# Narrower TensorE tiles, explicit PSUM banks, weights in long rows and a new written order in a retention-and-token-mixing kernel

## The chip, the cores and the metric

The kernel runs on one core of a Trainium2 chip. A core has a matrix engine (TensorE, PE in the profile, with its weight loads shown apart as PEld), a vector engine (DVE), a scalar engine (ACT), a general engine (GpSimd, POOL) and a sync engine (SP), which here only issues transfers. Sixteen DMA engines move data between HBM and SBUF. TensorE writes its results to PSUM, eight banks of 2 KB in each of 128 partitions, and DVE and ACT read them from there. Each engine works through its own queue in order, and waits for the others by semaphores. The metric is the device time of one launch in microseconds (us).

## The reference

The first half is a recurrent attention with decay (retention), for 4 batches, 8 heads, 768 steps and head width 64; the second half mixes tokens within a batch. Cut to what is computed:

```python
gamma = 1.0 - 2.0 ** (-5.0 - arange(H))
for t in range(S):
    state = gamma * state + outer(k[:, :, t], v[:, :, t])
    y[:, :, t] = (1/sqrt(D)) * q[:, :, t] @ state
x = y with heads side by side                    # [4, 768, 512]
wq = x @ w_q;  wk = x @ w_k                      # 512 -> 64 each
W_tok = (1/sqrt(64)) * wq @ wk.T                 # [768, 768] in each batch
out = relu(W_tok @ x) @ w_out                    # 512 -> 512
```

All inputs and the output are float32 in HBM: q, k and v of 6.29 MB each, 1.31 MB of weights, and 6.29 MB of output.

## The kernel before, in words

**Work units.** The 768 steps of a batch are cut into three pieces of 256 steps, called pairs (two chunks of 128), so there are twelve pairs, 0 to 11, three to a batch. Partition g of a tile holds two neighbouring steps, j = 0 and 1, and the eight heads are handled as two halves x = 0, 1 of four head pairs hp each. All matrix products take bfloat16 operands.

**Retention, for each pair p.** Transfers bring k, q and v in 512 KB pieces into staging tiles (`load`). `ck`, `cq` and `cv` turn them into bfloat16, the first two with the decay multiplied in (L253). `trk` and `trq` transpose k and q on TensorE, eight 128x128 transposes each, and `ekT`, `eqT` copy the result out of PSUM. `sc` makes the scores of half of the heads (16 matmuls on 64x64 tiles of the array, L316), and `eat` multiplies them by the causal mask on DVE (L329). `ia` applies the masked scores to v (L422). `st`, `X`, `Y` and `YS` add k times v into the state's PSUM bank and apply q to the state of the chunk before (L385), two streams of matmuls interleaved. `es` copies the state out. When the y of a pair is complete, `ex` copies it out of PSUM as x (L435).

**Token mixing.** W_tok is never formed: since W_tok @ x = wq @ (wk.T @ x), the kernel makes z = wk.T @ x once for each batch. `xt` and `exT` transpose x and copy it out. `wqk` makes wq (transposed, four matmuls of 256 columns, L460, with w_q in the stationary operand twice, so that the result stands on both halves of the partitions) and wk (eight matmuls of 64 columns, L470); `ew` copies both out. `zm` makes z from the three pairs of a batch (L492), so it can't run before the third pair's wk; `ez` copies it out. For each pair, `mx` multiplies z and wq (four matmuls of 256 columns, L514) into two banks, `r` applies the relu bank by bank (L529, L531), `pj` multiplies by w_out (four matmuls of 512 columns for each j, L538), and `eo` copies the result out for the store.

**Order.** The program's order is a written list of steps, ORDER (L17). A step's letter names its engine: A for ACT, V for DVE, P for POOL; steps without a letter are TensorE's. The list fixes the order within each engine's queue, and the framework adds the semaphores. `fill.n` puts n matmuls on zeros ahead of a step, whose result is overwritten; they keep TensorE busy. Loads and stores are both in SP's queue: the load of pair p+6 is issued when pair p's tile of the same name has been converted (`release`, L166), and the store of a pair where its second `eo` stands in the list. Both are in program order in that one queue. The three weight loads come after pair 2's loads (L159): w_q and w_k in 256-byte rows, w_out in rows of 2 KB.

**PSUM.** Of the eight banks, scores hold two, y two, the state one, and three rotate among all other results (L120 to L123).

Of the kernel before, what the change touches and what calls it, by code (L numbers as in the profile page):

```python
# [15 lines left out]

ORDER = """  # L17
fill.80 ck.0:V trk.0 cq.0:V ekT.0:A trq.0 cv.0:V fill.2 eqT.0:V
st.0 es.0.0:A sc.0.0 X.0 eat.0.0:V es.0.1:A sc.0.1 ck.1:P ia.0.0
eat.0.1:V cq.1:P Y.0 trk.1 fill.6 ekT.1:A ia.0.1 ex.0:V cv.1:P  # L20
trq.1 eqT.1:A xt.0 st.1 sc.1.0 exT.0:V ck.2:P es.1.0:A eat.1.0:V
X.1 es.1.1:A sc.1.1 cq.2:P trk.2 eat.1.1:V ia.1.0 ekT.2:V Y.1
ia.1.1 cv.2:A ex.1:V trq.2 st.2 fill.4 eqT.2:V xt.1 es.2.0:A
W:V sc.2.0 exT.1:A X.2 wqk.0 eat.2.0:V wqk.1 WO:A ew.0:V
sc.2.1 ew.1:V ia.2.0 eat.2.1:V ck.3:P Y.2 ia.2.1 ex.2:A cq.3:P
trk.3 xt.2 ekT.3:A fill.4 exT.2:V cv.3:A wqk.2 trq.3 ew.2:A
st.3 eqT.3:V zm.0 ck.4:P es.3.0:A ez.0:A X.3 sc.3.0 es.3.1:A
mx.0 eat.3.0:V r.0.1:A cq.4:P trk.4 r.0.0:A sc.3.1 ekT.4:A ia.3.0
eat.3.1:V mx.1 Y.3 r.1.0:A pj.0.0 cv.4:P r.1.1:A trq.4 fill.4
eo.0.0:A st.4 eqT.4:V ia.3.1 ck.5:P pj.0.1 ex.3:A es.4.0:V sc.4.0  # L30
eo.0.1:A X.4 eat.4.0:V xt.3 es.4.1:V cq.5:P trk.5 ekT.5:A exT.3:V
pj.1.0 sc.4.1 eo.1.0:A cv.5:P trq.5 eat.4.1:V ia.4.0 mx.2 eqT.5:A
YS.4 ia.4.1 es.5.0:A ck.6:P r.2.0:A ex.4:V wqk.3 trk.6 r.2.1:A
sc.5.0 pj.1.1 ew.3:A eat.5.0:V cq.6:P eo.1.1:A X.5 ekT.6:V ia.5.0
sc.5.1 cv.6:A xt.4 eat.5.1:V trq.6 pj.2.0 exT.4:A eqT.6:V ck.7:P
YS.5 eo.2.0:A sc.6.0 es.6.0:A ia.5.1 eat.6.0:V wqk.4 cq.7:P ex.5:A
pj.2.1 ew.4:A trk.7 eo.2.1:V xt.5 ekT.7:V sc.6.1 X.6 exT.5:V
cv.7:A eat.6.1:V trq.7 ia.6.0 eqT.7:A wqk.5 ck.8:P es.6.1:A sc.7.0
ew.5:V YS.6 eat.7.0:V es.7.0:A ia.6.1 zm.1 ex.6:A cq.8:P sc.7.1
ez.1:V X.7 eat.7.1:V trk.8 es.7.1:A xt.6 ekT.8:V cv.8:A ia.7.0  # L40
trq.8 exT.6:V Y.7 st.8 eqT.8:V mx.3 es.8.0:A ia.7.1 ck.9:P
r.3.1:A r.3.0:V sc.8.0 ex.7:V wqk.6 eat.8.0:V pj.3.0 ew.6:A cq.9:P
trk.9 eo.3.0:A pj.3.1 ekT.9:V X.8 eo.3.1:A cv.9:P mx.4 sc.8.1
r.4.0:A r.4.1:V trq.9 eat.8.1:V pj.4.0 eqT.9:A ck.10:P ia.8.0 eo.4.0:V
mx.5 YS.8 r.5.1:A r.5.0:V sc.9.0 ia.8.1 es.9.0:V pj.4.1 cq.10:P
ex.8:V trk.10 eo.4.1:A eat.9.0:V pj.5.0 ekT.10:A trq.10 cv.10:A eo.5.0:V
sc.9.1 X.9 eat.9.1:V ia.9.0 xt.8 ck.11:P xt.7 eqT.10:A exT.7:V
pj.5.1 exT.8:V wqk.7 es.9.1:V cq.11:P eo.5.1:A trk.11 ew.7:A wqk.8
YS.9 ew.8:V cv.11:P ekT.11:A sc.10.0 ia.9.1 es.10.0:A eat.10.0:V trq.11
ex.9:A zm.2 eqT.11:V X.10 ez.2:A sc.10.1 es.10.1:A ia.10.0 eat.10.1:V  # L50
mx.6 YS.10 r.6.0:A xt.9 es.11.0:A r.6.1:A sc.11.0 exT.9:V ia.10.1
mx.7 eat.11.0:V pj.6.0 r.7.0:A ex.10:V r.7.1:A wqk.9 eo.6.0:A pj.6.1
ew.9:A X.11 eo.6.1:A sc.11.1 ia.11.0 eat.11.1:V mx.8 pj.7.0 r.8.0:A
r.8.1:A Y.11 eo.7.0:V ia.11.1 pj.7.1 ex.11:A eo.7.1:A xt.10 xt.11
exT.10:V pj.8.0 exT.11:V wqk.10 eo.8.0:A wqk.11 ew.10:A pj.8.1 ew.11:A
zm.3 eo.8.1:A ez.3:A mx.9 r.9.0:A r.9.1:V mx.10 pj.9.0 r.10.1:A
r.10.0:V eo.9.0:V pj.9.1 mx.11 eo.9.1:A r.11.1:V r.11.0:A pj.10.0 eo.10.0:A
pj.10.1 eo.10.1:A pj.11.0 eo.11.0:A pj.11.1 eo.11.1:A
""".split()

STAGES = 6
# [3 lines left out]
def kernel(  # L65
# [10 lines left out]


# [10 lines left out]
    C = 128  # L88
# [15 lines left out]

# [3 lines left out]
    ost_pool = pool("ost", 7)  # L108
# [8 lines left out]
    moe_pool = pool("moe", 6)  # L117
    relu_pool = pool("relu", 2)
    PSUM = bass.MemoryType.PSUM
    at_psum = pool("at_psum", 1, space=PSUM)  # L120
    y_psum = pool("y_psum", 1, space=PSUM)
    s_psum = pool("s_psum", 1, space=PSUM)
    psum = pool("psum", 3, space=PSUM)  # L123

    pairs = [dict() for _ in range(NG)]
    state_ps = [None] * B
# [13 lines left out]
    def load(name, p):  # L140
        src = {"k": k, "q": q, "v": v}[name]
        b, cp = divmod(p, NP)
        t = stage_pool.tile([128, H, 2, D], FP32, name=name + "_st")
        eng = nc.scalar if (name, p) == ("k", 0) else nc.sync
        eng.dma_start(
            out=t.rearrange("g h j d -> g h (j d)"),
            in_=src[b, :, cp * 2 * C : (cp + 1) * 2 * C, :].rearrange(
                "h (g j) d -> g h (j d)", j=2
            ),
        )  # L150
        pairs[p][name + "_st"] = t

    wq_stage = wstage_pool.tile([128, NDM, DH], FP32, name="wq_stage")
    wk_stage = wstage_pool.tile([128, NDM, DH], FP32, name="wk_stage")
    wout_stage = wstage_pool.tile([128, NDM, DM], FP32, name="wout_stage")
    for p in range(STAGES):
        for name in "kqv":
            load(name, p)
        if p == 2:  # L159
            nc.sync.dma_start(out=wq_stage, in_=moe_w_q.rearrange("(a p) h -> p a h", p=128))  # L160
            nc.sync.dma_start(out=wk_stage, in_=moe_w_k.rearrange("(a p) h -> p a h", p=128))
            nc.sync.dma_start(
                out=wout_stage, in_=moe_w_out.rearrange("(a p) m -> p a m", p=128)
            )

    def release(name, p):  # L166

        if p + STAGES < NG:
            load(name, p + STAGES)
# [27 lines left out]

# [20 lines left out]
    wq_sb = const_pool.tile([128, NDM, 2, DH], BF16, name="wq_sb")  # L218
# [3 lines left out]
    def W(e):  # L222
        copy(
            e,
            wq_sb,
            wq_stage[:, :, None, :].to_broadcast([128, NDM, 2, DH]),
        )
        if e == "A":
            nc.scalar.mul(out=wk_sb, in_=wk_stage, mul=float(wk_scale))
        else:  # L230
            ENGINES[e].tensor_scalar_mul(out=wk_sb, in0=wk_stage, scalar1=float(wk_scale))
# [4 lines left out]


    fills = [0]

    def filled(dst):  # L240
        for i in range(fills[0]):
            if dst.dtype == BF16:
                nc.tensor.transpose(dst, warm, identity)  # L243
            else:
                nc.tensor.matmul(out=dst, lhsT=warm, rhs=warm, start=True, stop=True)
        fills[0] = 0
# [3 lines left out]
    def decay(e, p, name, table):  # L250
        st = pairs[p]
        st[name + "s"] = cast_pool.tile([128, HP, 2, 2, D], BF16, name=name + "s")
        ENGINES[e].tensor_tensor(  # L253
            out=st[name + "s"].rearrange("p hp j x d -> p x (hp j) d"),
            in0=st[name + "_st"].rearrange("p (x hp) j d -> p x (hp j) d", x=2),
            in1=table[:, p % NP]
            .rearrange("p (x hp) j -> p x (hp j)", x=2)
            .to_broadcast([128, 2, HP * 2, D]),
            op=ALU.mult,
        )  # L260
        release(name, p)

    def ck(e, p):
        decay(e, p, "k", fk)

    def cq(e, p):
        decay(e, p, "q", fq)
# [345 lines left out]
```

## Time and profile before

| | |
|---|---|
| median of 3 runs (lowest to highest) | 112.1 us (110.33 to 112.9) |
| profiled execution, its span | 109.7 us |
| what the span leaves to the median | 2.4 us |
| TensorE busy, weight loads busy | 93.8 us, 68.9 us |
| DVE, ACT, POOL busy | 64.9, 60.0, 49.4 us |
| moved by the DMA engines | 26.77 MB, mean 244 GB/s |
| first decay of pair 0's k starts | 6.46 us |
| decay of pair 3's k starts | 24.56 us |
| z of batch 0 ends on TensorE | 35.55 us |
| last matmul ends | 105.17 us |

The profile is of one execution, and its durations belong to the span of 109.7 us, from the first to the last instruction. The time of a run holds, beside the span, what lies around it: the median of the runs shown is 2.4 us above this span. In the profile, "L538" is a line of the kernel. A row of the groups gives the operation, the tile written and the tiles read, their sizes and how many; then busy time, the mean of one in ns, the engine's idle time just before them, and what ended that. The slices cut the span into 40 parts of 2.74 us; a digit is the busy share in tenths, for PEclk the granted TensorE clock. The chain is the work that ended last, followed back step by step. A row of the waits gives who waited, for what, the total in us, how often, and the longest.

The durations of the rows that are spoken of below, one instruction each: the decay of k or q 1.90 us on POOL and 1.22 on DVE; the mask multiply 1.22 (DVE); a copy of a whole transposed pair 1.02 (ACT) or 0.69 (DVE); `ex` 1.01 (ACT) or 1.22 (DVE), six on each; `es` 0.37 (ACT) or 0.41 (DVE); `ew` 0.48 or 0.56; `ez` 0.37 or 0.43; one of the two relus of a pair 0.60 or 0.69; `eo` 0.59 or 0.69.

### The profile page before, as it was taken

The page shows a single profiled execution, that of the slowest core. Times are in us where ns is not written, and L with a number is a line of the kernel's source. Part 1 is how long each engine was busy: PE and PEld are TensorE (multiplying, and loading weights), DVE is VectorE, ACT ScalarE, POOL GpSimd, SP SyncE. Part 2 cuts the span into 40 slices and gives each one's busy share as a digit, 9 for nine tenths or more (in the row PEclk, how much of TensorE's full clock was granted, in tenths as well). Part 3 has the DMA queues.
Part 4 walks back from the last instruction along what each step waited for, and adds up shares of the span by engine and source line. Part 5 has one row for each costly group of instructions (what it writes and reads, how often), then busy time and mean ns, then how long its engine had stood idle before and what let it go on. Part 6 is the DMA issues. An engine that isn't in the chain of part 4 may idle for free.

```text
span 109.7 us, 4707 instructions
## 1 busy us (share of the span) xinstructions
PE 93.8 (85%) x2132; PEld 68.9 (63%) x2132; DVE 64.9 (59%) x87; ACT 60.0 (55%) x94; POOL 49.4 (45%) x41
## 2 busy tenths in 40 slices
PE   3999596994579899999998959999999999958930
PEld 3998485783458576667687837557787647633400
DVE  1066756894422665687688849799857954225100
ACT  5004137265273975958848515549587866554640
POOL 6405968008699996968229999321000000000000
PEclk9999958999967999999999999999999999999999
DMA  1999999999999999999999999824040022430471
GB/s 38 309 347 346 342 342 238 313 334 306 289 327 337 345 344 304 339 337 333 287 297 281 300 354 370 332 115 166 31 197 0 6 87 111 191 158 33 191 312 73
DMA packets 40917, 26.77 MB, mean 244 GB/s; under 512 B 1857, under 2 KB 38721, under 8 KB 40897
## 3 DMA queue, kind: packets, MB, share of 16 engines
q1 hardware_dynamic: 39856, 25.96, 75.0%
q10 hardware_dynamic: 1040, 0.52, 1.6%
q8 instruction: 16, 0.26, 0.9%
q14 instruction: 5, 0.03, 0.1%
HBM read 20.19 MB, written 6.29 MB: 241 GB/s over the span
## 4 chain that ended last, share of the span: by engine, by line
PE 78%; DVE 10%; issue 5%; ACT 3%; POOL 1%; POOLq 0%; DVEq 0%; ACTq 0%
PE o_ps L538 20%; PE at_ps L316 8%; PE y_ps L422 6%; PE ktr_ps L243 6%; PE xt_ps L445 6%; DVE at_sb L329 6%; PE wqk_ps L460 6%; PE qtr_ps L299 6%; PE y_ps L385 5%; PE ktr_ps L285 3%; PE z_ps L492 3%; PE wqk_ps L470 3%; PE mx_ps L514 3%; PE state_ps L385 2%; DVE xT L133 1%
## 5 line engine op out<-in xcount | busy, mean ns | idle before, releaser
L329 DVE TENSOR_TENSOR at_sb<-at_ps,cmask 128x1024 bf16<-128x1024 f32 x24 | 29.3, 1222 | 9.5 <-PE at_ps L316 9.3
L253 POOL TENSOR_TENSOR ks<-k_st,fk 128x1024 bf16<-128x1024 f32 x11 | 20.9, 1902 | 19.0 <-DMA k_st<-in_k_dram 14.8
L538 PE MATMUL o_ps<-wout_sb,relu 128*128 128x512 bf16 x96 | 24.1, 380 | 0.3 <-ACT o_st L132 0.3
L253 POOL TENSOR_TENSOR qs<-q_st,fq 128x1024 bf16<-128x1024 f32 x11 | 20.9, 1902 | 1.2 <-DMA q_st<-in_q_dram 1.2
L132 ACT COPY o_st<-o_ps 128x512 f32<-128x512 f32 x19 | 11.1, 586 | 9.9 <-PE o_ps L538 9.8
L316 PE MATMUL at_ps<-qT,kT 64*64 64x128 bf16 x384 | 10.6, 221 | 4.0 <-DVE at_sb L329 2.3
L538 PEld LDWEIGHTS <-relu 128*128 128x128 bf16 x96 | 8.2, 98 | 8.0 <-issue 1.2
L132 ACT COPY kT<-ktr_ps 128x1024 bf16<-128x1024 bf16 x7 | 7.1, 1015 | 9.9 <-PE ktr_ps L285 9.9
L529 ACT ACTIVATE relu<-mx_ps 128x512 bf16<-128x512 f32 x18 | 10.2, 598 | 3.3 <-PE mx_ps L514 2.6
L316 PEld LDWEIGHTS <-kT 64*64 64x64 bf16 x384 | 7.1, 106 | 6.7 <-issue 5.6
L132 ACT CAST s_sb<-state_ps 128x256 bf16<-128x256 f32 x16 | 6.0, 373 | 8.8 <-PE state_ps L385 8.7
L385 PE MATMUL y_ps<-s_sb,qT 64*64 64x64 bf16 x320 | 9.6, 195 | 1.0 <-DVE at_sb L329 1.0
L133 DVE COPY xT<-xt_ps 128x1024 bf16<-128x1024 bf16 x10 | 6.7, 686 | 6.1 <-PE xt_ps L445 6.1
L385 PEld LDWEIGHTS <-qT 64*64 64x64 bf16 x320 | 7.2, 108 | 4.7 <-issue 2.7
L385 PE MATMUL state_ps<-vs,ks 64*64 64x64 bf16 x320 | 8.9, 194 | 1.5 <-issue 1.4
L422 PE MATMUL y_ps<-vs,at_sb 64*128 64x64 bf16 x384 | 10.0, 193 | 0.2
L243 PEld LDWEIGHTS <-warm 128*128 128x128 bf16 x90 | 7.7, 129 | 1.9 <-DVE warm L174 1.1
L422 PEld LDWEIGHTS <-at_sb 64*128 64x128 bf16 x384 | 7.2, 96 | 2.6 <-DVE at_sb L329 0.5
L132 ACT CAST x_nat<-y_ps 128x1024 bf16<-128x1024 f32 x6 | 6.1, 1012 | 4.7 <-PE y_ps L422 4.6
L243 PE MATMUL ktr_ps<-identity,warm 128*128 128x128 bf16 x80 | 7.0, 275 | 1.9 <-POOL identity masks.py:199 1.9
L385 PEld LDWEIGHTS <-ks 64*64 64x64 bf16 x320 | 6.9, 109 | 2.4 <-issue 2.1
L531 DVE TENSOR_SCALAR relu<-mx_ps 128x512 bf16<-128x512 f32 x6 | 4.2, 692 | 7.1 <-PE mx_ps L514 7.1
(57 smaller groups left out, 137.5 us busy)
## 6 DMA issues: line engine op xcount, KB each, us to landing
q_st<-in_q_dram SPq DMA_DIRECT2D x12, 512.0 KB, 6.7
v_st<-in_v_dram SPq DMA_DIRECT2D x12, 512.0 KB, 6.5
k_st<-in_k_dram SPq DMA_DIRECT2D x11, 512.0 KB, 6.7
out_dram<-o_st SPq DMA_DIRECT2D x11, 512.0 KB, 2.7
wout_stage<-in_moe_w_out_dram SPq DMA_DIRECT2D x1, 1024.0 KB, 7.0
k_st<-in_k_dram ACTq DMA_DIRECT2D x1, 512.0 KB, 5.6
out_dram<-o_st SPq DMA_DIRECT2D x2, 256.0 KB, 2.8
wq_stage<-in_moe_w_q_dram SPq DMA_DIRECT2D x1, 128.0 KB, 5.4
```

Source lines behind the costliest of these rows:

```text
L132: return nc.scalar.copy(out=out, in_=in_)
L133: return ENGINES[e].tensor_copy(out=out, in_=in_)
L243: nc.tensor.transpose(dst, warm, identity)
L253: ENGINES[e].tensor_tensor(out=st[name + "s"].rearrange("p hp j x d -> p x (hp j) d"), in0=st[name + "_st"].rearrange("p (x hp) j d -> p x ...
L299: nc.tensor.transpose(ps[:, hp, :, j, :], st["qs"][:, hp, j], identity)
L316: nc.tensor.matmul(out=ps[rows(c), x, hi, j, :], lhsT=st["kT"][rows(x), hp, j, c, :], rhs=st["qT"][rows(x), hp, c, :], start=(hi == 0 and ...
L329: st["eat", half] = ENGINES[e].tensor_tensor(out=st["at", half].rearrange("p x hi j t -> p (x hi) (j t)"), in0=st["at_ps", half].rearrange ...
L385: out.append(nc.tensor.matmul(skip_group_check=True, **mm))
L422: nc.tensor.matmul(out=st["y_ps"][:, c, x, hp, :], lhsT=st["at", half][rows(c), x, hi, j, :], rhs=st["vs"][rows(c), hp, j, x, :], start=(( ...
L445: nc.tensor.transpose(ps[:, a, c, :], st["x"][:, c, a * 128 : (a + 1) * 128], identity)
L529: nc.scalar.activation(out=dst, in_=src, func=ACT.Relu)
L538: nc.tensor.matmul(out=ps, lhsT=st["relu"][:, a, j], rhs=wout_sb[:, a, :], start=(a == 0), stop=(a == NDM - 1),)
```

## The change

**Loads.** k of pair 0 comes as two halves, one from ACT's queue and one at the head of SP's. All 36 loads share one ring of 18 staging tiles, in an order LOADS that has w_q and w_k after pair 2 and w_out after pair 5; a load is issued once the tile 18 places before it has been converted. The weights are laid so that partition p holds rows 4p to 4p+3 of the matrix, which makes one long row of 1 KB (w_q, w_k) or 8 KB (w_out) in each partition. x is permuted in the same way: `ex` writes feature 4n+a to column n of block a. Stores are held back until every load has been put into the queue, and ten output tiles take the place of seven.

**TensorE.** `wqk` puts wq of chunk c on partitions 64c to 64c+63 (eight matmuls of 128 columns with a 64-column stationary operand) and makes wk as sixteen matmuls with 64-column stationary operands. Its output is 256 columns wide, and was 384. z is copied to both halves of the partitions, with all 512 columns, by four copies a batch (`ez` twice, two copies in each). `mx` is sixteen 64x64 matmuls of 128 columns into two banks, and `r` one relu over both. `fill` is a step of its own, with ordinary matmuls.

**PSUM.** All eight banks are one tensor, and each step names its bank after an @; scores, y and the mixed result take two neighbours. The state is in bank 7.

**Order.** ORDER is new throughout. w_q and w_k are converted on POOL, w_out on DVE. Pair 3's retention, and part of pair 4's, stands before batch 0's `zm`; at the end, eleven of the 24 `pj` stand after batch 3's.

```diff
+LOADS = "q0 v0 k1 q1 v1 k2 q2 v2 w k3 q3 v3 k4 q4 v4 k5 q5 v5 o k6 q6 v6 ...
-STAGES = 6
+STAGES = 18
+OBUFS = 10
...
 ORDER (start, around batch 0's zm, and end)
+cv.0:A ck.0.0:P ck.0.1:V cq.0.1:V fill.70@6 trk.0@6 cq.0.0:P fill.11@0 trq.0@0 st.0 ekT.0:V
+es.0.0:A eqT.0:V sc.0.1@0 sc.0.0@2 cq.1:P cq.2:P ck.1:V X.0@4 fill.4@6 trk.1@6 ekT.1:A es.0.1:V
+fill.22@6 trq.1@6 eat.0.1:V eat.0.0:V cv.1:V eqT.1:A ia.0.1 YS.0 ia.0.0 es.1.0:A W:P ck.2:V
...
+ck.4:P sc.2.1@0 wqk.0@6 cq.3:V xt.1@2 ew.0:A X.2@4 trk.3@6 exT.1:A trq.3@2 ia.2.0 eqT.3:A
+eat.2.1:V ia.2.1 st.3 es.3.0:A ekT.3:V sc.3.0@2 cq.4:P ck.5:P X.3@0 eat.3.0:V Y.2 cq.5:P wqk.1@6
+sc.3.1@2 ia.3.0 es.3.1:V ew.1:V ex.2:A trk.4@4 xt.2@6 eat.3.1:V cv.4:A exT.2:V ia.3.1 trq.4@5
+wqk.2@6 YS.3 ekT.4:A ew.2:A eqT.4:V es.4.0:A sc.4.1@4 eat.4.1:V zm.0@6 ex.3:A cv.5:P sc.4.0@2
+trk.5@0 xt.3@1 eat.4.0:V X.4@4 exT.3:V ez.0.0:A ez.0.1:A mx.0@2 es.4.1:V trq.5@6 ekT.5:A eqT.5:V
+mx.1@0 ia.4.1 ia.4.0 r.0:A YS.4 WO:V sc.5.1@2 wqk.3@6 r.1:A ex.4:A sc.5.0@0 xt.4@4 ck.6:P
...
+wqk.10@0 eo.5.0:A eo.8.1:A ew.11:A mx.6@2 ew.10:A r.6:A mx.7@4 zm.3@6 pj.8.0@0 ez.3.1:V r.7:V
+pj.6.0@1 pj.6.1@2 eo.6.0:V ez.3.0:A pj.7.0@6 eo.6.1:A mx.10@2 mx.9@4 eo.8.0:V eo.7.0:A mx.11@0
+r.10:A pj.7.1@6 pj.10.1@2 r.11:V pj.10.0@3 pj.11.1@0 eo.7.1:A pj.11.0@6 eo.10.1:V eo.10.0:V
+r.9:A pj.9.0@1 pj.9.1@4 eo.9.0:A eo.9.1:A eo.11.1:V eo.11.0:V
...
-    at_psum = pool("at_psum", 1, space=PSUM)
-    y_psum = pool("y_psum", 1, space=PSUM)
-    s_psum = pool("s_psum", 1, space=PSUM)
-    psum = pool("psum", 3, space=PSUM)
+    psum = pool("psum", 1, space=bass.MemoryType.PSUM)
+    banks = psum.tile([128, 8, 512], FP32, name="banks")
...
-            nc.sync.dma_start(out=wq_stage, in_=moe_w_q.rearrange("(a p) h -> p a h", p=128))
+            nc.sync.dma_start(out=wq_stage, in_=moe_w_q.rearrange("(p a) h -> p a h", a=NDM))
...
+    load("k", 0, 0, nc.scalar)
+    load("k", 0, 1, nc.sync)
...
+    def more_loads():
+        while queue:
+            token, _, half = queue[0].partition("/")
+            if token not in "wo" and token not in staged:
+                n = len(staged)
+                if n >= STAGES and staged[n - STAGES] not in cast:
+                    return
+                staged.append(token)
+            load_token(queue.pop(0))
...
-        copy(e, st["x"], st["y_ps"].rearrange("p c x hp d -> p c (x hp d)"))
+        for_c = st["y_ps"].rearrange("p c x hp (d4 a) -> p c (x hp d4) a", a=NDM)
+        copy(e, st["x"].rearrange("p c a n -> p c n a"), for_c)
...
     def wqk
-        ps = psum.tile([128, 2 * C + 2 * DH], FP32, name="wqk_ps", tag="ps")
+        ps = bank32(b)[:, 0:256]
         for a in range(NDM):
+            for c in range(2):
                 nc.tensor.matmul(
+                    out=ps[rows(c), 0:C],
+                    lhsT=wq_sb[:, a, :],
+                    rhs=st["xT"][:, a, c, :],
...
+        for c in range(2):
+            for a in range(NDM):
+                for u in range(2):
+                    nc.tensor.matmul(
+                        out=ps[rows(u), C + c * DH : C + (c + 1) * DH],
+                        lhsT=st["xT"][:, a, c, u * G : (u + 1) * G],
+                        rhs=wk_sb[:, a, :],
...
+        for half in range(2):
+            copy(e, z_sbs[bt][rows(r), half * 256 : half * 256 + 256], ps[rows(half), :])
...
     def mx
+        for a in range(NDM):
+            for u in range(2):
+                for c in range(2):
+                    nc.tensor.matmul(
+                        out=ps[rows(u), c, a, :],
+                        lhsT=z[rows(c), a * 128 + u * 64 : a * 128 + u * 64 + 64],
+                        rhs=st["wqk"][rows(c), 0:C],
...
+        if not queue:
+            while stores:
+                store(*stores.pop(0))
```

## The prediction

> **What bounds the kernel now.** I read the page's busy times and 40 slices first, for who is full and when.
>
> ```profile
> span 109.7 us, 4707 instructions
> ...
> PE 93.8 (85%) x2132; PEld 68.9 (63%) x2132; DVE 64.9 (59%) x87; ACT 60.0 (55%) x94; POOL 49.4 (45%) x41
> ...
> PEclk9999958999967999999999999999999999999999
> DMA  1999999999999999999999999824040022430471
> ```
>
> TensorE is busiest. The DMA engines are full until slice 26 (71 us), and the clock falls to 5 and 6 tenths twice, both before 36 us. So I ask next who waited for transfers, and when, in the waits and the timeline.
>
> ```profile
> POOL ks L253 <- DMA k_st<-in_k_dram: 14.8, 6, 5.7
> ```
>
> ```profile
> 15.87 0.69 SPq L162 DMA_DIRECT2D wout_stage<-in_moe_w_out_dram  x1
> ...
> 24.56 1.90 POOL L253 TENSOR_TENSOR ks<-k_st,fk 128x1024 bf16<-128x1024 f32 x1 [5.73 <-DMA k_st<-in_k_dram]
> ```
>
> The longest wait, 5.7 us, is pair 3's k: the 1 MB of w_out was queued ahead of it. Pairs 4, 7 and 8 also start on their transfer (29.66, 43.81, 48.50 us). Last I read the chain in order of time, for what a full TensorE takes per step (start, duration, matmuls).
>
> ```profile
> 32.15 1.01 PE wqk_ps L460 x4
> ...
> 42.00 0.35 PE at_ps L316 x16
> ...
> 45.70 0.22 PE mx_ps L514 x4
> ...
> 82.19 0.78 PE z_ps L492 x12
> ...
> 94.06 0.44 PE wqk_ps L460 x4
> 94.50 0.23 PE wqk_ps L470 x8
> ```
>
> Between 9 and 36 us the chain often leaves TensorE (1.24 at 11.11, 1.40 at 25.67, 1.24 at 27.37, 1.02 at 29.47, 0.70 at 31.40, 1.24 at 36.19), and the first wqk line takes twice its warm 0.44. From 36 to 105 us nearly every piece is a matmul. So: starved early, TensorE-bound later. Batch 0's z ends at 35.55 us, TensorE at 105.17, the last eviction at 105.76, the span at 109.72.
>
> **What the Trainium skill says.** "TensorEngine Tiling (Array Packing)", Key Properties: a change of tiling mode drains the array. The trace agrees: eight transposes take 0.45 us before their like and 0.55 before a 64-row step, 0.10 a drain. "TensorE: Matmul & The Clock Gate", Part 3, The mechanism: matmuls on different row and column groups run concurrently. It agrees: sixteen 64x64 matmuls of 128 columns take 0.35 us, 22 ns each, where one on the whole array takes 56 (0.45/8). "SBUF — State Buffer", Specifications: lines are 16 bytes, and each crossing to a new line "pays a penalty"; no row of this trace writes 2-byte elements to a new line each time.
>
> **The loads.** 512 KB at the 342 GB/s of slices 5 and 6 is 1.53 us. k2 lands by 15.06 us. After it now come q2, v2, the two small weights (0.26 MB, 0.8) and k3: 15.06+3x1.53+0.8 = 20.4 us, 4.2 before today's 24.56. k4 follows at 25.0 (today 29.66), k5 at 29.6; then w_out's 3.07 us, and k6 at 37.2 against 39.06. Long weight rows matter only inside this: slice 7 shows 238 GB/s, 0.8 us lost at most, already in the 4.2. The first load in two halves ahead of q0 lets k0 land after 0.5 MB and not among 1 MB: 1.5 us sooner, of which fills (80 in 7.00 us, now 70 and 11) and q0, v0, landing as before, leave about 0.5. Stores now stand behind all loads on SP: nothing waits for them but ten output buffers, and loads are queued before the first eviction.
>
> **Up to batch 0's z.** The 4.2 us shifts it from 35.55 to 31.4. But the new order puts pair 3's remaining score, state and y steps, pair 4's transposes and one score step before it, 3.4 us of TensorE work (three sc 0.35, two ia 0.34, two state/y 0.37, two transposes 0.45, one more sc). They go into gaps that the chain shows as 5.6 us between 25 and 37 us; two at_ps slots in place of one remove the wait of scores for the mask multiply (2.3 us). The vector engine gets 23.5 us of work by then (18.8 now; counts by their rows), which fits between 5 and 32. Two waits are new there. 22 fill matmuls in trk.1's bank wait for ekT.1 (ACT, 1.02), and behind them on TensorE stand trq.1, ia.0.1 and YS.0; cq.3 on DVE waits for q3 (20.4+1.5 = 21.9) ahead of eat.2.1, for which ia.2.1 waits. Each costs between nothing, if pair 0's mask multiplies and eat.2.0 last as long, and about 1 us. I leave 1.6 us for these, gaps that don't fill and a cold clock: z ends at 33.0. W moves to POOL ahead of ck.3 with no row to price it: 0.5 to 1.0 us by POOL's cast (1.04 per 1024 elements), hidden in the 1.5 us between the weights' landing and k3's; WO moves to DVE, 2x0.69, behind it eat.5.0, with sc and wqk of other pairs queued.
>
> **TensorE after z.** Left in the new order: 23 groups of transposes x0.45, 15 sc x0.35, 16 ia x0.34, 18 state/y x0.37, 9 wqk, 3 zm x0.78, 12 mx, 24 pj x0.86. wqk was 0.67 (0.44+0.23); now it is 8 matmuls of 128 columns and 16 of 64 on two column tiles. Fully overlapped: 8x27+16x22 ns = 0.57; not at all: 8x56+16x29 = 0.91. I take 0.62, as zm's column tiles overlap well (65 ns a matmul). mx becomes sixteen 64x64 matmuls of 128 columns, sc's own shape: 0.35, for 0.22 to 0.32. Sum 10.4+5.3+5.4+6.7+5.6+2.3+4.2+20.6 = 60.5, with 23 drains 62.8. The same sum for the old order is 63.5+2.7 = 66.2, while 105.17-35.55 = 69.6 passed, so 3.4 us of stalls; I give the new order 3.0. TensorE ends at 33.0+62.8+3.0 = 98.8.
>
> **Evictions.** ez becomes four 64x256 copies a batch (0.37 ACT, 0.43 DVE): +4.8 us of engine time, but two run on each engine, so z to mixing grows by 0.4, under pj.8.0 and pj.6 at the end (0.86 each); uncovered it costs 4x0.4. ew drops from 0.48 to 0.37, relu from 2x0.60 to one 1.01: off the path, with slack. ex now writes consecutive elements 128 columns (256 bytes) apart; its price is 1.01 (ACT) if the stride is free, up to double if each element pays. I take 1.01 and keep the other end for a rival. Explicit banks add no instruction; a step waits for its own bank's reader.
>
> **Tail.** The last eviction ends 0.6 after TensorE. Today 256 KB then remain and 3.96 us pass. Now pair 9's 512 KB is issued first and pair 11's two halves behind it: 0.75 MB more is 2.2 us at 342 GB/s if nothing overlaps, 0.5 (one more SP issue) if all does; I take 1.3. Sum: 98.8+0.6+5.3 = 104.7 us, 5.0 under the span of 109.7. The median of the runs is 112.1, 2.4 above that span; carried over, 107.1, so 107.0.
>
> **Rivals.** (a) Slower: the strided write of ex. Eleven stand in ACT's queue ahead of es, ekT, ez and relu, one on DVE; at double price 11x1.01+1.22 = 12.3 us. ACT's work between z of batches 0 and 1, 18.5 us, becomes 22.5 against TensorE's 21.5, so ACT paces. All on the path: 119; half: 113. It decides against the change from 0.6 us per ex on the path ((114.3-107.1)/12). For it: the skill's sentence; against: it speaks of absorbing access latency, and a write need not wait. (b) The early gain doesn't come: k3 is early but DVE or a cold clock holds z at 36.5: 110.6. For it: DVE's work before z grows by a quarter (three more decays and a cast, of pairs 1 to 3); against: those stand where it now waits for transfers. (c) Column tiles that don't overlap: 9x0.29 = 2.6 us, 109.7. (d) The forecast's own good end: no stalls, z at 31.4, a tail of 4.5: 31.4+62.8+0.6+4.5 = 99.3, or 101.7.
>
> **Chances.** The forecast, with (c) partly in it and (d): 0.62, its own range 102.5 to 109.8. (b) and full (c): 0.13, within 2%. (a): 0.25, of which 0.06 lands within 2% and 0.19 beyond. A measurement of this kernel tells 2% from no change, 109.9 to 114.3. Faster 0.62, same 0.19, slower 0.19. The range 102.5 to 114.5 leaves out most of (a)'s slow part and a little of (d).
>
> **What would show it.** k3's decay at 20 to 21 us, z of batch 0 done near 33, clock never under 8 tenths after 10 us; wqk about 0.6 in all, mx 0.35; x_nat on ACT at 1.01; TensorE done near 99 and 6 us from there to the end. x_nat near 2 us on ACT, with TensorE waiting for ACT, would make the prediction wrong on the slow side; TensorE idle between 33 and 75 us on banks would too.

## The result, and the profile after

| | before | changed |
|---|---|---|
| median of 5 runs each (lowest to highest) | 112.1 us (110.33 to 115.41) | 156.74 us (155.72 to 161.08) |
| ratio, 95% interval | | 1.4063 [1.3884, 1.4241] |
| profiled span | 109.7 us | 159.4 us |
| `ex` on ACT, one copy | 1.01 us | 4.72 us |

The changed kernel is 44.6 us slower. Runs of one kernel fall into a faster and a slower state, so medians here are of all runs and ratios with an interval compare the faster ones alone; the changed kernel was profiled in one of its slower runs, at a mean granted clock of 0.776, where the faster ones had 0.82 to 0.84. The reading rests on the duration of `ex`, which a copy alone at a granted clock of 1.0 repeats (e4: 4.73 us).

The page of the changed kernel, the parts that answer to those shown of before:

```profile
span 159.4 us, 5331 instructions
...
PE 112.4 (71%) x2433; PEld 85.4 (54%) x2433; DVE 73.1 (46%) x92; ACT 101.4 (64%) x92; POOL 43.8 (27%) x40
...
PEclk9999956755558586598589598796586968969996
DMA  3999999999999999960030000300003003030936
...
ACT x_nat L124 32%; PE banks L554 13%; PE banks L457 7%; PE banks L396 6%; PE banks L294 6%; PE banks L433 6%; PE banks L248 6%; PE banks L309 5%; DVE x_nat L125 3%; PE banks L330 3%; PE banks L531 3%; PE banks L472 2%; PE banks L504 1%; PE banks L483 1%; ACT kT L124 1%
...
L124 ACT CAST x_nat<-banks 128x1024 bf16<-128x1024 f32 x11 | 51.9, 4719 | 5.6 <-PE banks L396 3.5
```

ACT rose from 60.0 to 101.4 busy us, and more than half of that is one group: eleven `ex` copies at 4719 ns, 51.9 us (six took 6.1 before). The chain holds all twelve: its x_nat shares are 32.5% on ACT (L124) and 3.0% on DVE (L125), together 35.5% of 159.4, or 56.6 us, and 11x4.719+4.716 is 56.6. So the whole of every copy lies on the chain. The DMA row empties after slice 18 (72 us) because the last load has landed by then, at 70.12 us; before it was 69.00, so the loads are not what is late. The clock row falls to 5 and 6 tenths all along; in e1 below, which differs in this copy alone, it does so only between 25 and 35 us.

The waits of the changed kernel (who, for what: us in all, times, longest):

```profile
DVE xT L125 <- PE banks L457: 19.7, 5, 4.5
PEld L457 <- ACT x_nat L124: 19.5, 6, 4.0
...
PE banks L457 <- ACT x_nat L124: 17.9, 6, 3.8
```

Its chain in order of time, around batch 0's z (start, duration, what):

```profile
36.91 4.73 ACT x_nat L124
41.63 0.04 issue
41.67 1.01 PE banks L294 x8
42.69 0.85 PE banks L457 x8
...
47.03 4.62 ACT x_nat L124
51.65 0.04 issue
51.69 1.01 PE banks L294 x8
```

The transposes of k (L294), which are to be written to the bank that `ex` still reads, those of x (L457) and whatever stands behind them in TensorE's order wait for `ex`. Then eight transposes take 1.01 and 0.85 us where they took 0.45, with the granted clock at half. Here is rival (a) at more than twice the price that it was given.

### The profile page after: what moved, and what is told of

The parts are those of the page before. It is cut to its first block, busy times and chain, and to the rows that moved or that the text cites. A ratio compares the mean times of both kernels' runs of the same rounds, so it can differ in the third digit from the quotient of the medians.

```text
span 159.4 us, 5331 instructions
## 1 busy us (share of the span) xinstructions
PE 112.4 (71%) x2433; PEld 85.4 (54%) x2433; DVE 73.1 (46%) x92; ACT 101.4 (64%) x92; POOL 43.8 (27%) x40
## 4 chain that ended last, share of the span: by engine, by line
PE 58%; ACT 34%; DVE 3%; issue 1%; ACTq 0%
ACT x_nat L124 32%; PE banks L554 13%; PE banks L457 7%; PE banks L396 6%; PE banks L294 6%; PE banks L433 6%; PE banks L248 6%; PE banks L309 5%; DVE x_nat L125 3%; PE banks L330 3%; PE banks L531 3%; PE banks L472 2%; PE banks L504 1%; PE banks L483 1%; ACT kT L124 1%
## 5 line engine op out<-in xcount | busy, mean ns | idle before, releaser
L124 ACT CAST x_nat<-banks 128x1024 bf16<-128x1024 f32 x11 | 51.9, 4719 | 5.6 <-PE banks L396 3.5
L342 DVE TENSOR_TENSOR at_sb<-banks,cmask 128x1024 bf16<-128x1024 f32 x24 | 28.8, 1220 | 9.6 <-PE banks L330 8.9
L554 PE MATMUL banks<-wout_sb,relu 128*128 128x512 bf16 x96 | 28.0, 440 | 2.7 <-ACT x_nat L124 2.7
L457 PE MATMUL banks<-identity,x_nat 128*128 128x128 bf16 x96 | 11.6, 296 | 17.9 <-ACT x_nat L124 17.9
L260 POOL TENSOR_TENSOR ks<-k_st,fk 128x1024 bf16<-128x1024 f32 (+1 forms) x9 | 16.4, 1820 | 27.2 <-PE banks L396 18.6
L260 POOL TENSOR_TENSOR qs<-q_st,fq 128x1024 bf16<-128x1024 f32 (+1 forms) x9 | 17.0, 1888 | 15.4 <-DMA q_st<-in_q_dram 7.7
L457 PEld LDWEIGHTS <-x_nat 128*128 128x128 bf16 x96 | 9.1, 136 | 20.1 <-ACT x_nat L124 19.5
L124 ACT COPY o_st<-banks 128x512 f32<-128x512 f32 x17 | 10.6, 627 | 14.6 <-PE banks L554 14.6
L125 DVE COPY xT<-banks 128x1024 bf16<-128x1024 bf16 x7 | 4.8, 692 | 26.4 <-PE banks L457 19.7
L294 PE MATMUL banks<-identity,ks 128*128 128x128 bf16 x96 | 9.7, 265 | 9.5 <-ACT x_nat L124 9.5
L330 PE MATMUL banks<-qT,kT 64*64 64x128 bf16 x384 | 11.4, 252 | 3.4 <-DVE x_nat L125 3.2
L294 PEld LDWEIGHTS <-ks 128*128 128x128 bf16 x96 | 7.8, 120 | 10.7 <-issue 10.0
L396 PE MATMUL banks<-s_sb,qT 64*64 64x64 bf16 x320 | 11.4, 217 | 0.0
L433 PE MATMUL banks<-vs,at_sb 64*128 64x64 bf16 x384 | 11.1, 218 | 0.0
L125 POOL CAST vs<-v_st 128x1024 bf16<-128x1024 f32 x6 | 6.2, 1037 | 16.3 <-ACT s_sb L124 7.3
```

Source lines behind the costliest of these rows:

```text
L124: return nc.scalar.copy(out=out, in_=in_)
L125: return ENGINES[e].tensor_copy(out=out, in_=in_)
L260: ENGINES[e].tensor_tensor(out=st[name + "s"][:, :, :, xs].rearrange("p hp j x d -> p x (hp j) d"), in0=st[name + "_st"][:, xs].rearrange( ...
L294: nc.tensor.transpose(ps[:, hp, j], st["ks"][:, hp, j].rearrange("p x d -> p (x d)"), identity)
L330: nc.tensor.matmul(out=ps[rows(c), x, hi, j, :], lhsT=st["kT"][rows(x), hp, j, c, :], rhs=st["qT"][rows(x), hp, c, :], start=(hi == 0 and ...
L342: ENGINES[e].tensor_tensor(out=st["at", half].rearrange("p x hi j t -> p (x hi) (j t)"), in0=st["at_ps", half].rearrange("p (xhi jt) -> p ...
```

## The experiments

Each kernel ran beside the kernel before on the same chip. That one's medians there were 112.54 us (with e1 to e4), 112.86 (e5, e6, e8, e9) and 111.99 (e10 to e12), single runs from 109.11 to 119.85. The milestones that the readings below use, in us from the start of each profiled execution:

| | before | forecast | changed | e1 | e5 | e12 |
|---|---|---|---|---|---|---|
| decay of pair 3's k starts | 24.56 | 20 to 21 | 21.66 | 21.18 | 20.39 | 21.19 |
| batch 0's z ends | 35.55 | 33.0 | 47.84 | 37.31 | 35.07 | 36.93 |
| last matmul ends | 105.17 | 98.8 | 153.80 | 105.55 | 99.42 | 101.53 |
| span | 109.7 | 104.7 | 159.4 | 111.1 | 105.1 | 107.1 |
| median of the runs | 112.1 | 107.0 | 156.74 | 113.89 | 108.16 | 109.49 |

### e1: the same permutation, walked block by block

The same 1024 values go to the same places; only the order of the copy's walk changes, so that it writes without a break and reads PSUM every 16 bytes.

```diff
-        for_c = st["y_ps"].rearrange("p c x hp (d4 a) -> p c (x hp d4) a", a=NDM)
-        copy(e, st["x"].rearrange("p c a n -> p c n a"), for_c)
+        src = st["y_ps"].rearrange("p c x hp (d4 a) -> p c a (x hp d4)", a=NDM)
+        copy(e, st["x"], src)
```

> The changed kernel with one edit: the copy of y out of PSUM visits the elements block by block, so it reads every fourth float of PSUM (16 bytes apart) and writes x in unbroken rows; layouts and results are the same. Theory A, the scattered 2-byte write alone made the copy 4.72 us: the copy falls to 1.0 us on ACT and 1.2 on DVE, the clock stays at 0.95 or more, and the kernel comes to about 107 us. Theory B, the strided walk costs on whichever side it lies: the copy stays over 2 us and the kernel over 120 us. Theory C, the narrow tiles, the banks and the order cost on their own: the copy is short, and the kernel still takes 112 us or more.

Measured: 113.89 us (112.83 to 115.7), 1.0343 [1.0144, 1.0542] of before. On the page:

```profile
span 111.1 us, 5320 instructions
...
PEclk9999999995556999999999999999999999999998
...
q8 instruction: 19, 0.31, 1.0%
...
L124 ACT CAST x_nat<-banks 128x1024 bf16<-128x1024 f32 x11 | 11.2, 1017 | 3.7 <-PE banks L396 2.9
```

One edited statement gives back 42.9 us of median. So the scattered write is the regression. But the rest of the change is slower than before too, by 3.4%, where it was forecast 5 us faster: something else in it is wrong.

### e2: no permutation

Weights in the old row layout and x unpermuted, all else as changed.

```diff
-        for_c = st["y_ps"].rearrange("p c x hp (d4 a) -> p c (x hp d4) a", a=NDM)
-        copy(e, st["x"].rearrange("p c a n -> p c n a"), for_c)
+        src = st["y_ps"].rearrange("p c x hp d -> p c (x hp d)")
+        copy(e, st["x"].rearrange("p c a n -> p c (a n)"), src)
...
-            nc.sync.dma_start(out=wq_stage, in_=moe_w_q.rearrange("(p a) h -> p a h", a=NDM))
+            nc.sync.dma_start(out=wq_stage, in_=moe_w_q.rearrange("(a p) h -> p a h", p=128))
```

> The changed kernel without the permutation of x: the copy reads and writes unbroken rows, and the weights are loaded as before (256-byte and 2-KB rows), everything else as changed. Theory A: the copy is 1.01 us on ACT and 1.22 on DVE, and the kernel takes 107 us, up to 1 us more than with long weight rows and a short copy. Theory C (the rest of the change costs by itself): 112 us or more.

Measured: 115.6 us (113.47 to 116.51), 1.0395 [1.0026, 1.0765], with `ex` at 1.017 us as in e1. The permutation itself costs nothing that shows once it is read rather than written, and long weight rows are worth no more than the spread of the two.

### e3: the scattered write alone, in the kernel before

```diff
-        copy(e, st["x"], st["y_ps"].rearrange("p c x hp d -> p c (x hp d)"))
+        copy(
+            e,
+            st["x"].rearrange("p c (a n) -> p c n a", a=NDM),
+            st["y_ps"].rearrange("p c x hp (d4 a) -> p c (x hp d4) a", a=NDM),
+        )
```

and the three weights in long rows, as that permutation needs.

> The kernel before with one part of the change alone: x is written in the permuted layout, by the same scattered copy, and the weights in the matching long rows. Theory A: the copy takes 4.7 us on both engines where it took 1.01 on ACT and 1.22 on DVE, twelve times 3.6 us or 43 us in all; with six on each engine some of it is hidden: 135 to 157 us, and a clock under 0.9. Theory C (the copy is only part of the loss): under 130 us.

Measured: 162.76 us (162.37 to 165.41), 1.4815 [1.4588, 1.5042], worse than my upper bound of 157.

```profile
L132 ACT CAST x_nat<-y_ps 128x1024 bf16<-128x1024 f32 x6 | 28.3, 4716 | 5.4 <-PE y_ps L422 5.3
L133 DVE CAST x_nat<-y_ps 128x1024 bf16<-128x1024 f32 x6 | 28.3, 4712 | 2.9 <-PE y_ps L422 2.9
```

The two engines pay the same, 4716 and 4712 ns, so spreading the copies over both was no escape; the old order suffers as the new one does.

### e4 and e8: what a copy to scattered places costs by itself

Two kernels of copies alone, three of each form on ACT, DVE (from PSUM) and one on POOL (from SBUF, e4 only). Nothing ran beside them but POOL's, which overlapped DVE's last round. `flat` is 1024 float32 elements, `byn` the same ones taken as for `ex`.

```diff
+            copy(e, t_cont, flat)                                       # unbroken
+            copy(e, t_perm.rearrange("p c a n -> p c n a"), byn)        # ex of the changed kernel
+            copy(e, t_pad[:, :, :, 0:128].rearrange("p c a n -> p c n a"), byn)   # 260 bytes
+            copy(e, t_s4[:, :, 0], flat)                                # every 4 bytes
+            copy(e, t_8[:, :, 0], flat)                                 # every 8 bytes
+            copy(e, t_s16[:, :, 0], flat)                               # every 16 bytes
+            copy(e, t_s32[:, :, 0], flat)                               # every 32 bytes
+            copy(e, t_f32.rearrange("p c a n -> p c n a"), byn)         # float32, every 512 bytes
+            copy(e, t_rd, flat.rearrange("p (c n a) -> p c a n", c=2, a=4))  # read every 16 bytes
```

> No part of the reference is computed: a row of copies of 128x1024 elements into bfloat16, three of each form on ACT and then on DVE out of PSUM, and one of each on GpSimd out of SBUF, none beside another. Forms: unbroken (cont); the changed kernel's, neighbours 256 bytes apart in turns of four (perm), and 260 bytes apart (padd); every 4, 16 and 32 bytes (byfour, bysixteen, bythirtytwo); as perm into float32 (permf); in turns of 32, 64 bytes apart (square); read every 16 bytes, written unbroken (readstr); as perm out of SBUF (permsb). If each new 16-byte line costs: bysixteen, bythirtytwo, padd, square and permf are all about 4.7 us and byfour is short. If coming back to a line within four writes costs: perm and padd 4.7, bysixteen and bythirtytwo about 1.0. If writing half a 4-byte word costs: byfour is 4.7 too, and permf 1.0. If a power of two in the distance costs: padd is about 1.0, and bythirtytwo and square are long.

> No part of the reference is computed: the price of a copy by its write pattern, continued. Out of PSUM, on ACT and then on DVE, three of each: bfloat16 in runs of 2, 4 and 8 neighbours, each run 256 bytes from the one before in turns of four (runof2, runof4, runof8; 512 elements an instruction, the others 1024); bfloat16 every 8 bytes (byeight); float32 every 8, 16 and 32 bytes (fbyeight, fbysixteen, fbythirtytwo). If the price is one of each new 16-byte line, 4.6 ns for half a word: runs of 8 cost like an unbroken copy, runs of 4 up to twice that, byeight about 2.4 us, fbysixteen and fbythirtytwo 2.2 us and fbyeight about half of the excess. If a run that fills whole words escapes it, runof2 costs 1.1 us (half of 2.2) or less.

Groups of e4 (busy us, mean ns of one):

```profile
L50 ACT CAST padd<-src 128x1024 bf16<-128x1024 f32 x3 | 15.2, 5059 | 0.0
...
L50 ACT CAST perm<-src 128x1024 bf16<-128x1024 f32 x3 | 14.2, 4729 | 0.0
L50 ACT CAST bysixteen<-src 128x1024 bf16<-128x1024 f32 x3 | 14.1, 4711 | 0.0
...
L52 DVE CAST perm<-src 128x1024 bf16<-128x1024 f32 x3 | 14.1, 4702 | 0.0
...
L50 ACT COPY permf<-src 128x1024 f32<-128x1024 f32 x3 | 6.7, 2246 | 0.0
...
L54 POOL CAST perm<-zero 128x1024 bf16<-128x1024 f32 x1 | 4.7, 4732 | 3.6 <-DVE perm L52 3.6
...
L50 ACT CAST readstr<-src 128x1024 bf16<-128x1024 f32 x3 | 4.1, 1381 | 0.0
L50 ACT CAST cont<-src 128x1024 bf16<-128x1024 f32 x3 | 3.8, 1259 | 0.2 <-PE src L46 0.2
```

Copies of 1024 elements, mean us of one:

| write | ACT | DVE | ns per 16-byte line (ACT) |
|---|---|---|---|
| bfloat16, unbroken | 1.26 | 1.40 | 9.8 |
| bfloat16, every 4 bytes (four to a line) | 1.66 | 1.52 | 6.5 |
| bfloat16, every 8 bytes (two to a line) | 2.59 | 2.40 | 5.1 |
| bfloat16, every 16 bytes (one to a line) | 4.71 | 4.69 | 4.6 |
| bfloat16, every 32 bytes; 256; 260 bytes | 4.81; 4.73; 5.06 | 4.69; 4.70; 4.92 | 4.7; 4.6; 4.9 |
| float32, every 8 bytes (two to a line) | 1.33 | 1.24 | 2.6 |
| float32, every 16; 32; 512 bytes | 2.13; 2.22; 2.25 | 1.93; 1.97; 2.12 | 2.1; 2.2; 2.2 |
| bfloat16, unbroken, read every 16 bytes | 1.38 | 1.43 | |

The durations overlap: a copy can start 0.5 us before the one ahead has ended. The first unbroken copy on ACT, with none ahead, took 1.01 us, as in the kernels; the next two, each behind a scattered one, 1.37 and 1.39. So up to 0.4 us of a row can belong to the copy ahead.

A 2-byte write that opens a new 16-byte line costs about 4.6 ns, 4-byte writes about 2.1 ns, on ACT and DVE from PSUM and on POOL from SBUF alike (POOL: 4.73 and 2.23 us). One form stands out: DVE with its source in SBUF made the same scattered bfloat16 write in 2.71 us (twice; a third, beside POOL, took 6.27), where ACT took 4.78. So not every such write costs 4.6 ns; what makes the difference was not tested. The distance beyond 16 bytes, a power of two or not, and whether the line comes back later, change little. None of the causes set down before e4 fits alone: every 4 bytes is short though it writes half words, and a new line costs float32 half as much. Groups of two, four or eight neighbours, each group 256 bytes from the last, cost hardly more than unbroken ones: six such copies of 512 elements, two of each kind, took 3.04 to 3.28 us together on ACT, 0.51 to 0.55 for each, where half of an unbroken copy of 1024 is 0.50 to 0.70. Four bytes at a time are enough here. Reading PSUM every 16 bytes costs nothing that matters (1.38 against 1.26), which is why e1 works; the one strided read from SBUF on POOL took 4.42 us.

### e5 and e12: wide tiles in the new order

e1 with `wqk`, `z` and `mx` as before the change; order, banks, loads and the one relu stay. e12 is the same kernel again, on another chip.

```diff
-            for c in range(2):
...
-                    out=ps[rows(c), 0:C],
-                    lhsT=wq_sb[:, a, :],
-                    rhs=st["xT"][:, a, c, :],
+            nc.tensor.matmul(
+                out=ps[:, 0 : 2 * C].rearrange("p (j c g) -> p j c g", j=2, c=2),
+                lhsT=wq_sb[:, a].rearrange("p o h -> p (o h)"),
+                rhs=st["xT"][:, a].rearrange("p c (j g) -> p j c g", j=2),
...
-                        lhsT=z[rows(c), a * 128 + u * 64 : a * 128 + u * 64 + 64],
-                        rhs=st["wqk"][rows(c), 0:C],
+                    lhsT=z[rows(half), ai, :],
+                    rhs=st["wqk"][rows(half), 0 : 2 * C],
```

> The changed kernel with the unbroken copy of y (as in the first experiment) and the wide tiles of the kernel before put back in wqk, z and mixing: 12 and 4 matmuls a pair where it has 24 and 16, one copy of z a batch, 4293 TensorE instructions and not 4868; banks, loads and order stay as changed. Theory D, the many small matmuls outrun the 16-KB instruction transfers (19 where the kernel before has 16) and TensorE stands with nothing to wait for, about 8 us in the first experiment against 3.6 before: these gaps halve, and the kernel gains 3 to 5 us on the first experiment, to 109 to 111. Theory E, what is lost beside the copy is the slow clock of 25 to 36 us, a matter of the order: the kernel stays within 1.5 us of the first experiment, unless the clock changes too.

> The kernel of the wide-tiles experiment once more, for its interval against the kernel before: the order, loads and banks of the change without the scattered copy and the narrow tiles. From that experiment, 4 to 6% faster than before, 106 to 109 us.

Measured: 108.16 us (105.74 to 110.24) beside 112.86, and 109.49 (106.54 to 110.17) beside 111.99: medians 4.2% and 2.2% below before. The wide tiles are 5.7 us of median better than e1 (4.4 in e12; each on a chip of its own), although their matmuls take no less: in e1's chain a narrow `wqk` is 0.34+0.25 and `mx` 0.35, in e5's a wide one 0.54+0.23 and 0.33. What differs is this, in the two timelines of TensorE (start, duration; in brackets the idle time before, put down to "issue", that is, to no one):

```profile
39.05 0.21 PE L531 MATMUL banks<-wqk_sb,z_sb 64*64 64x128 bf16 x1
40.68 0.41 PE L531 MATMUL banks<-wqk_sb,z_sb 64*64 64x128 bf16 x15 [1.41 <-ACT kT L124]
...
57.87 0.39 PE L554 MATMUL banks<-wout_sb,relu 128*128 128x512 bf16 x1
60.74 0.59 PE L554 MATMUL banks<-wout_sb,relu 128*128 128x512 bf16 x2 [2.48 <-issue]
...
70.73 0.25 PE L531 MATMUL banks<-wqk_sb,z_sb 64*64 64x128 bf16 x3 [1.98 <-issue]
...
86.47 0.36 PE L330 MATMUL banks<-qT,kT 64*64 64x128 bf16 x11 [1.39 <-issue]
```

Those are e1's, with two more (1.60 at 23.46 and 1.14 at 44.68), 10.0 us together. The one at 40.68 is put down to a copy of k, but it splits a running step, which does not read k, just as the others do. e5's timeline has three, 4.2 us:

```profile
23.96 0.41 PE L396 MATMUL banks<-s_sb,qT 64*64 64x64 bf16 x15 [1.26 <-issue]
...
33.89 0.41 PE L330 MATMUL banks<-qT,kT 64*64 64x128 bf16 x15 [1.30 <-issue]
...
40.09 0.33 PE L433 MATMUL banks<-vs,at_sb 64*128 64x64 bf16 x11 [1.69 <-issue]
```

They split running steps: one matmul of three, three of sixteen, one of sixteen. That is hardly a semaphore's doing, as a step's operands are all there when its first matmul runs. Ahead of each of these nine stops a 16 KB transfer of the instruction queue had just landed: e1's from 58.20 to 59.07 us, its matmuls going on at 60.74; e5's from 31.51 to 32.39, going on at 33.89. The restart follows 1.3 to 1.7 us after the landing in all nine. The queues of e1's DMA engines in the stretch from 58.1 to 59.2 us (kind: packets, MB, share):

```profile
q1 hardware_dynamic: 690, 0.35, 105.9%
q8 instruction: 1, 0.02, 5.0%
```

q1, the loads, fills the engines while that transfer runs. The instruction queue moved 19 such blocks for e1's 4868 TensorE instructions (matmuls and weight loads as written) and 16 for e5's 4293: 256 instructions or so to a block. Counting the traces' matmuls and weight loads in order of start shows that the stops stand at the ends of blocks: e1's six are 768, 256, 767, 509 and 1021 instructions apart, e5's three 512 and 256, which are multiples of 256 but for the few records that a trace lacks (11 of e1's matmuls). So TensorE runs out of instructions where a block was fetched too late, and more and smaller matmuls use blocks up sooner. Most of the transfers do no harm.

How long TensorE stops differs from one execution to the next: e12, the program of e5, has seven stops of 0.4 to 2.0 us, 6.1 together, at ends of blocks too. Against e1's 10.0 us that leaves 5.8 of the 6.0 us of span between e1 and e5, and 3.9 of the 4.0 between e1 and e12.

### e9: narrow tiles in the kernel before

The edit of e5 the other way round, on the kernel before (4843 TensorE instructions).

```diff
-        ps = psum.tile([128, 2 * C + 2 * DH], FP32, name="wqk_ps", tag="ps")
+        ps = psum.tile([128, 256], FP32, name="wqk_ps", tag="ps")
...
+            for c in range(2):
...
+                    out=ps[rows(c), 0:C],
+                    lhsT=wq_sb[:, a, :],
```

> The kernel before with one part of the change alone: wqk, z and mixing on the changed kernel's narrow tiles (4843 TensorE instructions and not 4266; four copies of z a batch), its order and loads as they were, x written as before. Theory D: 2 to 5 us slower than the kernel before, as TensorE gaps with no releaser. My first reckoning (TensorE time the same within 1 us, extra copies hidden): within 1 us of the kernel before.

Measured: 119.78 us (117.53 to 121.34), 1.051 [1.0367, 1.0653]. The instruction queue moved 19 blocks as in e1 (16 before), and the stops of 0.3 us and more at ends of blocks grew from 3.1 us (1.40, 1.35, 0.31) to 6.6. Two of them in e9's timeline:

```profile
26.35 0.38 PE L468 MATMUL wqk_ps<-wk_sb,xT 128*64 128x64 bf16 x13 [1.59 <-issue]
...
62.62 0.30 PE L312 MATMUL at_ps<-qT,kT 64*64 64x128 bf16 x5 [1.60 <-issue]
```

In either order, then, narrow tiles cost some 5 us. In the new order nearly all of it is stops; of e9's 6.1 us of span 3.5 are. The rest I can't place; the further copies of z in each batch (four in place of one) are in it.

### e10: fewer instructions elsewhere

e5 with the filling matmuls a quarter as many and four times as long (4127 instructions), to see whether stops go with the count.

```diff
-        for _ in range(n):
+        for _ in range((n + 3) // 4):
...
-                out=bank32(b)[:, 0:128], lhsT=warm, rhs=warm, start=True, stop=True
+                out=bank32(b), lhsT=warm[:, 0:128], rhs=warm, start=True, stop=True
```

> The wide-tiles kernel with its fill matmuls of 128 columns replaced by a quarter as many of 512 columns: the same fill time, 83 fewer matmuls and as many fewer weight loads, 4127 TensorE instructions and not 4293. Theory D (TensorE stops when a 16-KB block of instructions is used up before the next has landed, and starts 1.2 to 1.7 us after it has): one transfer fewer, the blocks end at other places, and the three stops of 1.3, 1.3 and 1.7 us move or go: 0 to 3 us faster. Rival, the stops belong to the steps at which they were seen: they stay at the same steps, and the time is the same within 0.5 us.

Measured: 110.32 us (107.76 to 111.48), no gain over e12's 109.49 on the same chip. The stops did not go; they moved (0.60 at 35.85, 2.06 at 41.50, 2.17 at 65.07, 0.70 at 84.09), with the same 16 blocks, and come to 5.5 us beside e12's 6.1. The rival, that stops belong to steps, is refuted: counted as above, two of e5's stops stand before instructions 1470 (a score step) and 1726 (masked scores by v), and two of e10's before 1468 (state by q) and 1724 (a score step). These are the same places in the count but other steps, as e10 has fewer fills ahead of them. Its other two stops follow 1020 and 1022 instructions further on. That fewer instructions are faster, this run does not show.

### e6 and e11: w_out's place

e6 moves only w_out's load in the kernel before, behind pair 5, with its conversion later on DVE; e11 is e5 with w_out back behind pair 2.

```diff
-W:V sc.2.0 exT.1:A X.2 wqk.0 eat.2.0:V wqk.1 WO:A ew.0:V
+W:V sc.2.0 exT.1:A X.2 wqk.0 eat.2.0:V wqk.1 ew.0:V
...
-eat.3.1:V mx.1 Y.3 r.1.0:A pj.0.0 cv.4:P r.1.1:A trq.4 fill.4
+eat.3.1:V WO:V mx.1 Y.3 r.1.0:A pj.0.0 cv.4:P r.1.1:A trq.4 fill.4
```

> The kernel before with one part of the change alone: the 1 MB of w_out is loaded after pair 5 and not after pair 2, and converted on DVE just ahead of batch 0's first mixing steps (on ACT, early, before). The forecast's first term alone: pair 3's decay starts 3 us sooner, at 21.5 us, and as much of it as the rest of the order can use comes off, 1 to 3 us, so 109 to 111 us. Rival: the chain of masks and copies paces the start: no change within 1 us.

> The wide-tiles kernel with w_out loaded where the kernel before has it, behind pair 2 and the small weights, and not behind pair 5; nothing else moves. If the early arrival of pairs 3 to 5 is what the new order lives on (the forecast's 4.2 us), k of pair 3 comes 3.1 us later and the kernel is 2 to 4 us slower, 110 to 112 us. Rival: the order alone gains and the loads don't pace it: within 1 us of the wide-tiles kernel.

e6 measured 115.43 us (114.71 to 120.06), 1.0251 [1.0143, 1.0358]. Pair 3's decay starts 3.5 us sooner, at 21.01, and the old order can't use it: the sooner POOL runs, the sooner it meets DVE. The timeline of e6:

```profile
22.87 1.90 POOL L251 TENSOR_TENSOR qs<-q_st,fq 128x1024 bf16<-128x1024 f32 x1
22.94 2.11 DVE L133 CAST wq_sb<-wq_stage 128x512 bf16<-128x512 f32 x1
```

W's conversion on DVE takes 2.11 us, ending just after POOL's decay, where it took 0.42 before. The Trainium skill, "SBUF — State Buffer", Who interferes with whom, has DVE and GpSimd sharing a port pair under an exclusive lock; this pair of lines agrees. `wqk.0` waits 1.37 us for it. The late WO on DVE, which I placed, also holds the first `pj` to 41.45 us (38.61 before), so e6 prices the load's move together with my order.

e11 measured 110.51 us (108.11 to 112.14, 20 runs), 0.9801 [0.9738, 0.9864] of before, with pair 3's decay back at 24.99 us and z at 39.52. It is 1.0 us above e12 by the medians and 1.6 by the lowest runs, less than either spreads, so between the 2 to 4 us of the one reading and the 1 of its rival it doesn't decide. The earlier arrival of pair 3, on which the forecast's first 4.2 us stood, is worth some 1 to 2 us here.

## Why the prediction was wrong

**Evictions: the step that failed.** "I take 1.01 and keep the other end for a rival", with "up to double if each element pays". It measured 4.72 us on ACT and DVE. The mechanism was named, the place was right (ACT in front of es, ekT, ez and relu, with TensorE waiting), and the sentence cited for it was the right one; the bound wasn't a bound. "Double" came from no row: no trace had a write of 2 bytes to a new line. With the measured price and the rival's own sum, all on the path, 107.1+11x3.70+3.49 = 151.3 us, and the narrow tiles' 5 or so bring it near the 156.74 measured. That nearness is partly luck: the sum leaves out the slower clock, and what of e1's other waits the copies hide. The argument against it, that "a write need not wait", is refuted by e4: the copy is the slower for the write, not for the read. The Trainium skill, "SBUF — State Buffer", Specifications, says that two hits a line are needed for full bandwidth. By these runs two 2-byte hits are not enough (2.59 us against 1.26); two 4-byte ones nearly are (1.33).

**TensorE after z: the matmuls right, their supply missed.** `wqk` at 0.62 was 0.59 and `mx` at 0.35 was 0.35 or less. Column tiles overlap, and rival (c) fell. But the stalls were taken at 3.0 us whatever the tiles, and narrow tiles raised them, by using up blocks of instructions sooner. From z to the last matmul e1 took 68.2 us; with wide tiles 64.4 (e5) and 64.6 (e12), against 65.8 forecast.

**Loads: right, and worth little.** Pair 3's decay came at 21.66 us (20 to 21 forecast), and at 20.39 to 21.19 in the mended kernels. What it was to bring did not follow: e11 puts it at 1 to 2 us.

**Up to batch 0's z: rival (b), in part.** Forecast 33.0; 37.31 in e1, 35.07 in e5, 36.93 in e12, hardly better than before's 35.55. For stops at ends of blocks there was no term: e5 has two ahead of z, 1.26 and 1.30 us, e12 three, 2.2 us, e1 one of 1.60; and e1 and e12 add a granted clock of half, from 25.2 to 35.4 and from 28.1 to 34.9 us, where the forecast had "never under 8 tenths". In e10, with the full clock and at most 0.45 us of such stops ahead of it, z ended at 33.55 us, so one run bears out the rest of that term. The kernel before has such a stop too: the 1.40 us at 25.67, which the prediction counts among the gaps to be filled, is "issue" in the chain and splits a score step into 11 and 5 matmuls at the end of a block, so it isn't idle time that another step could have used. The 3.4 us of work put ahead of z add up to 3.7 by their own terms. The rival's time, 110.6, is near e12's 109.49, but its cause is borne out in the clock alone.

**Tail: right.** 5.9 us were given from the last matmul to the end; 5.7 in e5, 5.6 in e1 and e12.

**The sum.** With the scattered write and the narrow tiles taken out, e5's span is 105.1 and e12's 107.1 us, against 104.7 forecast. This near hit is partly luck: z came 2 to 4 us later than forecast, and the stretch after it went 1.2 to 1.5 better. What gained came after z, 69.6 to 64.5 us; no run separates the order, the banks, the ring of loads and the single relu in it, and w_out's place has little share (e11: 63.5 us). e1's reading order with wide tiles beats both kernels; by e11, the same but for w_out, at least 1.4%.

## What to carry to other kernels

When a layout change permutes an eviction, permute the side that reads PSUM and write SBUF unbroken, or in groups of at least two neighbouring bfloat16 elements; and where no row prices a scattered write, measure a copy of it alone before taking "double" as its upper end. Count TensorE's instructions as well as its matmul time: splitting tiles cut the time a little and added 13% instructions, at about 5 us. A load that lands sooner pays only if the order behind it and the engines that share ports can take it.

## What the runs showed that I had not expected

- A 2-byte write to each new 16-byte line costs 4.6 ns and a 4-byte one 2.1 ns, nearly the same on ACT and DVE out of PSUM and on POOL; the distance from one to the next changes little. DVE out of SBUF took 2.71 us for what cost 4.7 elsewhere.
- TensorE stops in the middle of a step, up to 2.5 us at a time, restarting 1.2 to 1.7 us after a 16 KB instruction transfer lands, in the kernel before as in e1, e5, e9, e10 and e12, and within one execution the stops lie multiples of 256 instructions apart, but for missing records. That these transfers queue among the loads on busy DMA engines is seen; that they are late because of it was not tested, and it can't be the whole cause: e1's stop at 86.47 us follows a transfer from 84.14 to 85.11 us, when the one other queue at work took 2.4% of the DMA engines' time.
- A copy on the path also slows the engine that waits for it: in the changed kernel TensorE's own busy time rose from e1's 90.0 us to 112.4, for the same matmuls, with the granted clock at 5 to 8 tenths in most slices. The loss is not the sum of both: the twelve copies alone take 44.2 us more than e1's, and the median rose by 42.9.
